# Head-first lanes, T stored by lanes, and weight words moved to ACT's queue in a fused recurrence + two MoE kernel

## The chip, the cores and the metric

One core of a Trainium2 chip runs one program. Times are microseconds (us) on the device. Three runs of the kernel before took 1322.34, 1306.5 and 1322.2 us, median 1322.2. Engines are named as in the profile: PE (TensorE matmul) and PEld (its weight loads), DVE (VectorE), ACT (ScalarE), POOL (GpSimd), and SP, which here only issues DMAs. SP, ACT and POOL each have a queue of their own for the DMAs that they issue.

## The reference, cut to what matters

Three layers run one behind the other on 4 x 768 = 3072 tokens of 320 numbers (8 heads of 40).

```python
for t in range(S):                                   # S = 768, state (B, H, 40, 40) per head
    y[:, :, t] = einsum('bhd,bhde->bhe', rt, state)
    Sa = einsum('bhde,bhe->bhd', state, at)
    state_decay = state * wt[:, :, None, :] - einsum('bhd,bhe->bhde', Sa, bt)
    state = state_decay + einsum('bhd,bhe->bhde', vt, kt)
x = y as tokens (3072, 320)
h = x @ w_in; g = where(h > 0, h, exp(min(h, 0)) - 1); x = g @ w_out      # MoE 1: 320 -> 2048 -> 320
e = argmax(x @ w_gate); p = softmax(x @ w_gate)[e]                        # MoE 2: 8 experts, 320 -> 1024 -> 320
out = p * (relu(x @ w1[e]) @ w2[e])          # up to `capacity` tokens per expert
```

The weights of MoE 1 come as 64-bit numbers. The kernel loads their words and builds a 32-bit number, split in a high part and a low part, on the chip ("conversion").

## The kernel before, in words

**Attention in chunks.** The recurrence is computed in 24 chunks of 32 steps (C), two chunks to a pair p (12 pairs). There are 32 heads over the batch, so a *lane* is one head's 32 steps of one chunk: 128 lanes are the 32 heads of 4 chunks. `lanes(g)` (L126) prepares group g = 0..5, four chunks each: it loads w, a, b and k with 128 lanes on the 128 partitions, multiplies up the decays of w along the 32 steps (L161, L164), the inverse decays (L185, L188), scales a, b and k with them (L169, L191, L196) and stores the results in DRAM (scr_A, scr_W, scr_BK), from where they are read again token by token. Group 0 runs on DVE with room for all four inputs at once, its DMAs on SP's queue; groups 1 to 5 run on POOL with one buffer W and one buffer lx, their DMAs on POOL's queue.

**From lanes to T and U.** `load_tok` (L211) brings tokens of r, a and b/k into two buffers in a fixed order; `pre(p)` (L260) transposes them, multiplies a with b/k into the matrix T of each lane, masks it (L285) and stores it in DRAM (Td, L290). `inverse(p)` (L299) reads T of a pair with 64 lanes on the partitions (TL, L306) and inverts 1 - T in 31 dependent steps of three small DVE operations (L314, L319, L321), stores the inverse in DRAM (Ud, L325) and reads it back as UT (L328). `chain(c, put)` (L363) is the dependent work of a chunk: X from T and the state (copy L390), P from X and UT, the state's update, the output Y (L448), and its transposed tokens.

**MoE 1** (`block`, L567) takes a pair's 256 tokens through w_in and w_out, one pair behind the chain, and `Router.tile` ranks the tokens for MoE 2 and stores them as rows (L699). `Moe1.weights` (L486) makes 40 conversions, 8 times (two w_in tiles, one stacked w_in tile, two w_out tiles). In each, SP loads words into one of three buffers `raw` (L495), ACT takes the absolute value (L499), DVE does four operations (L500 to L503), ACT casts the high part, POOL subtracts it for the low part (L473 by `split`, L510). A w_out conversion is followed by transposes and by a matmul with w_gate on PE (L531, L535). **MoE 2** follows at the end; the change does not touch it.

**What sets the order.** The code is written as generators; `weave` takes steps from several in a given ratio, and a planner then orders the instructions of each engine by priority and by its own picture of time. `ahead(tc, g, n)` gives the steps of g a priority n earlier, `issue_after(i)` keeps a DMA or an instruction behind instruction i in the planner's order. Each engine then runs its list strictly in order, and so does each DMA queue's issuing engine. Before the change, the start (`start`, L1084: lanes 0, pre(0), the loads of chunk 0, lanes 1, the inverse of pair 0, pre(1)) is woven with all 40 conversions 100 to 60 (L1109), behind it comes the loop over pairs.

The dimension order of a lane load, before:

```python
def load(t, x):                                                        # L138
    queue.dma_start(
        flat(t), self.src[x][:, :, 128 * g:128 * g + 128, :].rearrange("b h (c s) d -> c (b h) (s d)", c=4))
```

Of the kernel before, what the change touches and what calls it, by code (L numbers as in the profile page):

```python
# [23 lines left out]
C = 32  # L24
# [14 lines left out]
class Attention:  # L39
# [7 lines left out]
    def __init__(self, ctx, tc, nc, r, k, v, w, a, b):  # L47
# [12 lines left out]
        self.Td = [dr([C, 64, C], f"Td{p}") for p in range(NP)]  # L60
# [65 lines left out]
    def lanes(self, g, eng, eng2=None, room=None):  # L126
# [11 lines left out]
        def load(t, x):  # L138
            queue.dma_start(
                flat(t), self.src[x][:, :, 128 * g:128 * g + 128, :].rearrange("b h (c s) d -> c (b h) (s d)", c=4))  # L140
# [7 lines left out]
        load(w, "w")  # L148
        load(la, "a")
        if room:  # L150
            load(lb, "b")
            load(lk, "k")
# [25 lines left out]
        v = ps[:, 0:128].rearrange("p (c i j) -> p c i j", c=4, j=2)  # L178
# [17 lines left out]
        nc.gpsimd.tensor_tensor(lk, lk, V[:, 1:33, :], ALU.mult)  # L196
# [13 lines left out]

    def load_tok(self):  # L211

        if self.loaded == len(self.order):
            return
        kind, i = self.order[self.loaded]
        t = self.t("tok", self.loaded)
        self.loaded += 1
        for hg in range(2):
            rows = t[64 * hg:64 * hg + 64]
            if kind == "r":  # L220
                self.load_heads(rows, self.src["r"], hg, 64 * i, 64)
            elif kind == "a":
                for cc in range(2):
                    lane = (2 * (i % 2) + cc) * 32 + 16 * hg
                    self.nc.sync.dma_start(
                        rows[32 * cc:32 * cc + 32, :, 0:40],
                        self.scr_A[i // 2][lane:lane + 16].rearrange("l s d -> s l d"))
            else:
                lane = (i % 4) * 32 + 16 * hg
                self.last = self.nc.sync.dma_start(  # L230
                    rows[:, :, 0:40], self.scr_BK[i // 4][lane:lane + 16].rearrange("l x d -> x l d"))
# [28 lines left out]
    def pre(self, p):  # L260
# [13 lines left out]
        for cc in range(2):  # L274
# [24 lines left out]
    def inverse(self, p):  # L299
# [4 lines left out]
        for i in range(2):  # L304
            half = slice(64 * i, 64 * i + 64)
            self.last = self.nc.sync.dma_start(TL[half], self.Td[p].rearrange("s l t -> l s t"))  # L306
            nc.vector.memset(UL[half].rearrange("p a b -> p (a b)")[:, i::34], 1.0)
        yield
        for j in range(31):
# [10 lines left out]
            if m:  # L320
                nc.vector.tensor_tensor(UL[:, 0:n, j + 2:32], UL[:, 0:n, j + 2:32], tv, ALU.add)  # L321
# [15 lines left out]
    def load_bkd(self, c):  # L337
        for hg in range(2):
            lane = (c % 4) * 32 + 16 * hg
            self.nc.sync.dma_start(  # L340
                self.t("BKd", c)[64 * hg:64 * hg + 64], self.scr_BK[c // 4][lane:lane + 16].rearrange("l x d -> x l d"))

    def load_wp(self, c):
        for b in range(4):
            lane = (c % 4) * 32 + 8 * b
            self.nc.sync.dma_start(
                self.t("Wp")[32 * b:32 * b + 32].rearrange("p (h d) -> p h d", h=8),
                self.scr_W[c // 4][lane:lane + 8].rearrange("h s d -> s h d"))
# [127 lines left out]
class Moe1:  # L476
# [9 lines left out]
    def weights(self, pool, route):  # L486
# [5 lines left out]
        def convert(load, m, outs, stacked=False):  # L492
            raw = pool.tile([128, DM, 2], U32, tag="raw", name="raw", bufs=3)
            for q, src in load:
                nc.sync.dma_start(raw.rearrange("p n t -> p (n t)")[:, 0:2 * m].bitcast(U64)[q], src)  # L495
            hi, lo = raw[:, 0:m, 1], raw[:, 0:m, 0]
            xf = route.new_x2()[:, 0:m]
# [6 lines left out]
            if stacked:  # L504
# [10 lines left out]
        every = slice(0, 128)  # L515
        for j in range(FF // n):
            cs = slice(j * n, j * n + n)
            for kt in range(2):
                convert([(every, self.w_in[128 * kt:128 * kt + 128, cs])], n, (self.wiH[:, kt, cs], self.wiL[:, kt, cs]))
                yield  # L520
            convert([(slice(0, 64), self.w_in[256:320, cs]), (slice(64, 128), self.w_in[256:320, cs])], n,
                    (self.wiS[:, cs],), True)
            yield
            for f in (2 * j, 2 * j + 1):
                xf, t = convert([(every, self.w_out[128 * f:128 * f + 128, :])], DM,
                             (self.woH[:, f, 0:DM], self.woL[:, f, 0:DM]))
                with self.tc.high_priority(offset=500):
# [9 lines left out]
                    split(nc, self.woH[:, f, DM:], self.woL[:, f, DM:], ps[:, 384:384 + E])  # L537
                yield
# [78 lines left out]
class Router:  # L617
# [11 lines left out]
    def setup(self):  # L629
        nc, t = self.nc, self.c.tile  # L630
        self.wg = t([128, 3, E], F32, name="wg")
        nc.sync.dma_start(self.wg[:, 0:2, :], self.w_gate[0:256, :].rearrange("(k p) e -> p k e", p=128))
        nc.sync.dma_start(self.wg[0:64, 2, :], self.w_gate[256:320, :])
# [36 lines left out]
    def tile(self, c, o):  # L670
# [28 lines left out]
        nc.sync.dma_start(self.rows.rearrange("(b s) d -> b s d", b=B)[:, C * c:C * c + C, :], x2[:, 0:ROW])  # L699
# [347 lines left out]
def body(ctx, tc, r, k, v, w, a, b, w_in, w_out, w_gate, w1, w2, out, capacity=768):  # L1047
# [35 lines left out]

    def start():  # L1084
# [9 lines left out]
        att.load_pv(0)  # L1094
        att.load_bkd(0)
        att.load_pv(1)
        att.load_wp(0)
        with tc.issue_after(att.last.ins):
            drain(att.lanes(1, nc.gpsimd))
        yield from inverse  # L1100
        yield from att.pre(1)

    def some(g, n):
        for _ in range(n):
            if next(g, 0) == 0:
                return
            yield

    weave((ahead(tc, start(), 1000), 100), (conv, 60))  # L1109
# [90 lines left out]
```

## Time and profile before

| what | us |
|---|---|
| median of three runs | 1322.2 |
| profiled execution | 1325.83 |
| its span | 1324.0 |
| PE busy | 1037.8 |
| DVE busy | 802.2 |
| ACT busy | 598.3 |
| POOL busy | 299.6 |
| first moe1 matmul (L583) begins | 249.7 |
| X copies of the 24 chunks (L390), first and last | 139.7, 954.6 |

Busy time is an average over stages with different limits: it says which engine has the most to do, not what ends the waits in one stage. In a row of the timeline, the number behind the start is the duration, and in brackets stands the idle time of the engine before it with what ended it. In the chain of waits each row is a start, a duration and the work or the wait that held the chain there; "SPq" is SP's queue while it issues. The DMA share is the mean busy share of 16 DMA engines.

### The profile page before, as it was taken

What the parts mean: (1) busy time and instruction counts of PE and PEld (TensorE: products, weight loads), DVE (VectorE), ACT (ScalarE), POOL (GpSimd) and SP (SyncE); (2) the same over time, 40 slices, a digit from 0 to 9 for tenths busy, and PEclk for the clock granted to TensorE, in tenths of its full rate; (3) what the DMA queues carried; (4) which work ended last, traced back from release to release, by engine and by line L of the source; (5) the groups of instructions that cost most, each with busy time, mean ns of one, the idle gap of its engine ahead of it and who ended that gap; (6) DMA issues with size and microseconds to landing.
All of it is one profiled execution on the core that took longest, in us unless ns stands there. A gap on an engine that the chain in (4) does not pass through costs nothing.

```text
span 1324.0 us, 35742 instructions
## 1 busy us (share of the span) xinstructions
PE 1037.8 (78%) x14568; PEld 945.8 (71%) x14568; DVE 802.2 (61%) x2714; ACT 598.3 (45%) x1498; POOL 299.6 (23%) x355
## 2 busy tenths in 40 slices
PE   0144165777769988989899999989989679999994
PEld 0133155666668777878788888889989679889994
DVE  2345675677448864878667686867555425655541
ACT  0233123445425544546455655656656425534430
POOL 4343253454231341021000000000000141232311
PEclk9999996898779988899899999989999879999997
DMA  3767456655563566455452536342130146545210
GB/s 99 167 157 134 114 128 135 139 154 107 134 141 68 112 125 132 68 100 104 68 88 45 90 56 101 53 81 49 28 89 11 35 116 174 138 127 162 76 41 19
DMA packets 325645, 131.27 MB, mean 99 GB/s; under 512 B 292808, under 2 KB 307280, under 8 KB 325472
## 3 DMA queue, kind: packets, MB, share of 16 engines
q1 hardware_dynamic: 304848, 89.24, 34.4%
q0 software_dynamic: 19664, 37.43, 10.1%
q8 instruction: 117, 1.92, 0.7%
q10 hardware_dynamic: 960, 2.23, 0.6%
q14 instruction: 56, 0.46, 0.1%
HBM read 99.13 MB, written 31.00 MB: 98 GB/s over the span
## 4 chain that ended last, share of the span: by engine, by line
DMA 27%; PE 24%; DVE 23%; issue 11%; ACT 3%; POOL 3%; SPq 2%; another core or an unknown queue 0%; ACTq 0%; POOLq 0%; DVEq 0%
DMA W<-in_w_dram 5%; PE ps_h L583 4%; DMA out_dram<-ys,ids 4%; DVE ut L314 3%; DVE inv L319 3%; DMA inv<-Td 3%; DVE inv L321 3%; PE ps_c L375 3%; DMA lx<-in_k_dram 2%; DMA raw<-in_moe_w_in_dram 2%; DMA Ud<-inv 2%; DVE ST L421 2%; PE ps_c L903 2%; PE ps_h L903 2%; DVE e L589 2%
## 5 line engine op out<-in xcount | busy, mean ns | idle before, releaser
L472 ACT CAST gH<-e 128x256 fp32r<-128x256 f32 x192 | 77.0, 405 | 136.0 <-DVE e L589 128.4
L597 PE MATMUL ps_o<-woH,gH 128*128 128x328 f32 x384 | 130.2, 341 | 9.6 <-ACT gH L472 9.6
L599 PE MATMUL ps_o<-woH,gL 128*128 128x328 f32 x384 | 120.7, 336 | 8.3 <-DVE gL L473 8.2
L598 PE MATMUL ps_o<-woL,gH 128*128 128x328 f32 x384 | 126.0, 330 | 0.0
L583 PE MATMUL ps_h<-xH,wiH 128*128 128x256 f32 x368 | 112.5, 307 | 13.4 <-DVE e L589 12.6
L700 POOL DMA_INDIRECT list<-ids,idx x24 | 24.6, 1026 | 429.9 <-DVE idx L698 322.0
L589 DVE SCALAR_TENSOR_TENSOR e<-e,ps_h 128x256 f32<-128x256 f32 x184 | 76.5, 417 | 60.5 <-ACT e L588 58.2
L314 DVE TENSOR_TENSOR ut<-inv 128x30 f32<-128x30 f32 (+4 forms) x360 | 95.1, 264 | 26.9 <-DMA inv<-Td 26.5
L583 PE MATMUL ps_h<-xL,wiH 128*128 128x256 f32 x368 | 109.7, 298 | 0.0
L583 PE MATMUL ps_h<-xH,wiL 128*128 128x256 f32 x368 | 109.0, 296 | 0.0
L473 DVE TENSOR_TENSOR gL<-e,gH 128x256 fp32r<-128x256 f32 x192 | 81.5, 429 | 30.2 <-ACT gH L472 26.8
L319 DVE SCALAR_TENSOR_TENSOR inv<-inv 128x1 f32<-128x1 f32 (+15 forms) x372 | 98.1, 264 | 0.5
L321 DVE TENSOR_TENSOR inv<-inv,ut 128x30 f32<-128x30 f32 (+4 forms) x360 | 96.0, 267 | 0.3
L587 ACT ACTIVATE e<-ps_h 128x256 f32<-128x256 f32 x184 | 70.7, 384 | 54.4 <-PE ps_h L583 35.2
L244 PE MATMUL ps_p<-ident,tok 128*104 128x128 f32 x288 | 55.5, 321 | 41.0 <-DMA tok<-scr_A 15.4
L583 PEld LDWEIGHTS ps_h<-xH,wiH 128*128 128x128 f32 x368 | 73.7, 201 | 18.7 <-DVE e L589 17.6
L597 PEld LDWEIGHTS ps_o<-woH,gH 128*128 128x128 f32 x384 | 77.6, 202 | 12.0 <-ACT gH L472 10.7
L599 PEld LDWEIGHTS ps_o<-woH,gL 128*128 128x128 f32 x384 | 73.8, 200 | 10.7 <-DVE gL L473 9.7
L588 ACT ACTIVATE e<-e 128x256 f32<-128x256 f32 x192 | 79.1, 416 | 4.1
L598 PEld LDWEIGHTS ps_o<-woL,gH 128*128 128x128 f32 x384 | 77.8, 203 | 0.2
L583 PEld LDWEIGHTS ps_h<-xL,wiH 128*128 128x128 f32 x368 | 74.6, 203 | 0.1
L583 PEld LDWEIGHTS ps_h<-xH,wiL 128*128 128x128 f32 x368 | 74.2, 202 | 0.0
(308 smaller groups left out, 2882.4 us busy)
## 6 DMA issues: line engine op xcount, KB each, us to landing
r<-in_moe_w_dram SPq DMA_DIRECT2D x15, 640.0 KB
tok<-scr_BK SPq DMA_DIRECT2D x48, 160.0 KB
BKd<-scr_BK SPq DMA_DIRECT2D x48, 160.0 KB
r<-in_moe_w_dram SPq DMA_DIRECT2D x7, 1024.0 KB
W<-in_w_dram POOLq DMA_DIRECT2D x10, 640.0 KB
scr_BK<-lx POOLq DMA_DIRECT2D x10, 640.0 KB
inv<-Td SPq DMA_DIRECT2D x24, 256.0 KB
raw<-in_moe_w_out_dram SPq DMA_DIRECT2D x16, 320.0 KB
```

What stands on the lines that cost most here:

```text
L314: nc.vector.tensor_tensor(tv, TL[:, j:j + 1, j + 2:32].to_broadcast([128, n, m]), UL[:, 0:n, j:j + 1].to_broadcast([128, n, m]), ALU.mult,)
L319: nc.vector.scalar_tensor_tensor(col, UL[:, 0:n, j], TL[:, j, j + 1:j + 2], col, ALU.mult, ALU.add)
L321: nc.vector.tensor_tensor(UL[:, 0:n, j + 2:32], UL[:, 0:n, j + 2:32], tv, ALU.add)
L472: split.last = nc.scalar.copy(H, x)
L473: return (low or nc.vector).tensor_tensor(L, x, H.bitcast(F32), ALU.subtract)
L583: nc.tensor.matmul(h, l, r, start=i == 0, stop=i == len(seq) - 1)
L587: nc.scalar.activation(e, h, AF.Relu, scale=-1.0)
L588: nc.scalar.activation(e, e, AF.Exp, scale=-1.0)
L589: nc.vector.scalar_tensor_tensor(e, e, -1.0, h, ALU.add, ALU.max)
L597: nc.tensor.matmul(o, gH[:, ts], self.woH[:, f], start=f == 0, stop=False)
L598: nc.tensor.matmul(o, gH[:, ts], self.woL[:, f], start=False, stop=False)
L599: nc.tensor.matmul(o, gL[:, ts], self.woH[:, f], start=False, stop=f == NF - 1)
```

## The change

The change does four things.

- A lane group puts the four chunks of one head on neighbouring partitions (lane = 4 * head + chunk instead of 32 * chunk + head). The loads of w, a, b and k then have (b h) as their slowest dimension; all later reads of scr_A, scr_W and scr_BK take every fourth lane (`of`). In group 0, w and b go on SP's queue, k and a on ACT's. Its scaling of k runs on DVE (`eng2`), not on POOL.
- T is kept in DRAM lane by lane (Td is 64 lanes, s, t), so that the scatter is in the store and not in the load. UT comes back in four loads for each chunk instead of one, and the rows of a routed tile go out in four stores instead of one.
- The words of the weights (and w_gate) are loaded on ACT's queue, three buffers ahead. The low part is subtracted on DVE, and every third conversion has a buffer of its own.
- The first three word loads are set behind ACT's copy that reads k; nine conversions stand behind the scaling of k, ahead of the first inverse, and 31 behind the end of the first inverse. pre(1) is woven with those 31.

```diff
-        self.Td = [dr([C, 64, C], f"Td{p}") for p in range(NP)]
+        self.Td = [dr([64, C, C], f"Td{p}") for p in range(NP)]
@@ lanes
-                flat(t), self.src[x][...].rearrange("b h (c s) d -> c (b h) (s d)", c=4))
+                flat(t), self.src[x][...].rearrange("b h (c s) d -> (b h) c (s d)", c=4))
...
-        load(w, "w")
-        load(la, "a")
         if room:
-            load(lb, "b")
-            load(lk, "k")
+            for q, t, x in ((nc.sync, w, "w"), (nc.sync, lb, "b"), (nc.scalar, lk, "k"), (nc.scalar, la, "a")):
+                q.dma_start(
+                    flat(t), self.src[x][...].rearrange("b h (c s) d -> (b h) c (s d)", c=4))
+            self.landed = nc.scalar.copy(self.t("WCd")[:, 40:41], lk[:, 0, 0:1])
+        else:
+            load(w, "w")
+            load(la, "a")
...
-        nc.gpsimd.tensor_tensor(lk, lk, V[:, 1:33, :], ALU.mult)
+        self.scaled = eng2.tensor_tensor(lk, lk, V[:, 1:33, :], ALU.mult)
...
+    def of(self, t, c, first, n):
+        return t.rearrange("(l c) s d -> c l s d", c=4)[c, first:first + n]
@@ load_tok
+                with self.tc.issue_after(self.returned.ins) if i == 4 else ExitStack():
+                    self.last = self.nc.sync.dma_start(
+                        rows[:, :, 0:40], self.of(self.scr_BK[i // 4], i % 4, 16 * hg, 16).rearrange("l x d -> x l d"))
@@ pre
-                    self.Td[p][:, 32 * cc + 16 * hg:32 * cc + 16 * hg + 16, :].rearrange("s l t -> s (l t)"),
-                    TM[64 * hg:64 * hg + 32, :])
+                    self.Td[p][32 * cc + 16 * hg:32 * cc + 16 * hg + 16].rearrange("l s t -> s l t"),
+                    TM[64 * hg:64 * hg + 32, :].rearrange("s (l t) -> s l t", t=C))
@@ inverse
-            self.last = self.nc.sync.dma_start(TL[half], self.Td[p].rearrange("s l t -> l s t"))
+            self.last = self.nc.sync.dma_start(TL[half], self.Td[p])
...
-            self.nc.sync.dma_start(
-                self.t("UT", 2 * p + cc).rearrange("p h t -> p (h t)"),
-                self.Ud[p][:, 32 * cc:32 * cc + 32, :].rearrange("s (b h) t -> b s (h t)", b=4))
+            for b in range(4):
+                h = 32 * cc + 8 * b
+                self.returned = self.nc.sync.dma_start(
+                    self.t("UT", 2 * p + cc)[32 * b:32 * b + 32], self.Ud[p][:, h:h + 8, :])
@@ Moe1.weights
-                nc.sync.dma_start(raw.rearrange("p n t -> p (n t)")[:, 0:2 * m].bitcast(U64)[q], src)
+                    nc.scalar.dma_start(raw.rearrange("p n t -> p (n t)")[:, 0:2 * m].bitcast(U64)[q], src)
...
-                nc.gpsimd.tensor_tensor(H[r], xf[r], Hs[r].bitcast(F32), ALU.subtract)
+                nc.vector.tensor_tensor(H[r], xf[r], Hs[r].bitcast(F32), ALU.subtract)
             else:
-                split(nc, *outs, xf, nc.gpsimd)
+                split(nc, *outs, xf)
@@ Router.tile
-        nc.sync.dma_start(self.rows.rearrange("(b s) d -> b s d", b=B)[:, C * c:C * c + C, :], x2[:, 0:ROW])
+        for b in range(B):
+            at = S * b + C * c
+            nc.sync.dma_start(self.rows[at:at + C, :], x2[C * b:C * b + C, 0:ROW])
@@ body
-    weave((ahead(tc, start(), 1000), 100), (conv, 60))
+    first = ahead(tc, start(), 1000)
+    for _ in range(26):
+        next(first)
+    with tc.issue_after(att.landed.ins):
+        next(conv)
+    weave((first, 20), (behind(att.scaled.ins, some(conv, 9)), 20))
+    weave((ahead(tc, att.pre(1), 1000), 10), (behind(att.inverted.ins, conv), 40))
```

The planner decides where the pieces land, so the order of three places is shown. SP's queue at the very start, before (names: inv, lx and keep hold w, a, then b and k; raw holds words):

```order
L139 DMA inv<-in_w_dram 128x1x1280
L139 DMA lx_144<-in_a_dram 128x1x1280
L139 DMA keep<-in_b_dram 128x1x1280
L139 DMA keep<-in_k_dram 128x1x1280
L632 DMA wg<-in_moe_w_gate_dram 128x2x8
L633 DMA wg<-in_moe_w_gate_dram 64x8
L495 DMA raw<-in_moe_w_in_dram 128x256 x2
L208 DMA pv_151<-in_v_dram 32x16x40 x2
L208 DMA pv_152<-in_v_dram 32x16x40 x2
L495 DMA raw<-in_moe_w_in_dram 64x256 x2
L145 DMA scr_A_89<-lx_144 64x1280 x2
```

and SP's queue now:

```order
L151 DMA inv<-in_w_dram 128x1x1280
L151 DMA keep<-in_b_dram 128x1x1280
L145 DMA scr_A_89<-lx_144 64x1280 x2
L145 DMA scr_BK_101<-keep 64x1280 x4
L233 DMA tok_149<-scr_A_89 32x16x40 x4
L681 DMA list<-BKd_175 128x200
L239 DMA tok_150<-scr_BK_101 64x16x40 x2
L145 DMA scr_W_95<-W_143 64x1280 x2
```

Two of the lane loads, w_gate, the words and the loads of v have left the head of SP's queue: the stores of lanes 0 and the first token loads follow directly. DVE at the end of lanes 0, before (x_240 and x_253 are conversions, L191 scales b):

```order
L188 TENSOR_TENSOR inv<-inv 128x320
L500 SCALAR_TENSOR_TENSOR x_240<-x_240,raw 128x256
L188 TENSOR_TENSOR inv<-inv 128x320
L500 SCALAR_TENSOR_TENSOR x_253<-x_253,raw 128x256
L501 TENSOR_SCALAR raw<-x_240 128x256
L188 TENSOR_TENSOR inv<-inv 128x320
L501 TENSOR_SCALAR raw<-x_253 128x256
L502 SCALAR_TENSOR_TENSOR x_240<-x_240,raw 128x256
L188 TENSOR_TENSOR inv<-inv 128x320
L502 SCALAR_TENSOR_TENSOR x_253<-x_253,raw 128x256
L503 SCALAR_TENSOR_TENSOR x_240<-raw,x_240 128x256
L191 TENSOR_TENSOR keep<-keep,inv 128x1280
```

and now (L201 scales k, x_324 is the first conversion):

```order
L190 TENSOR_TENSOR inv<-inv 128x4x40
L193 TENSOR_TENSOR inv<-inv 128x320 x4
L196 TENSOR_TENSOR keep<-keep,inv 128x1280
L201 TENSOR_TENSOR keep<-keep,inv 128x1280
L516 SCALAR_TENSOR_TENSOR x_324<-x_324,raw 128x256
```

The lane work of group 0 is now in one piece, and the first conversion begins behind it. DVE at the beginning of the first inverse, before:

```order
L314 TENSOR_TENSOR ut_179<-inv 128x30
L319 SCALAR_TENSOR_TENSOR inv<-inv 128x1
L502 SCALAR_TENSOR_TENSOR x_415<-x_415,raw 128x256
L321 TENSOR_TENSOR inv<-inv,ut_179 128x30
L314 TENSOR_TENSOR ut_180<-inv 128x29
L503 SCALAR_TENSOR_TENSOR x_415<-raw,x_415 128x256
L319 SCALAR_TENSOR_TENSOR inv<-inv 128x1
L473 TENSOR_TENSOR woL<-ps_r,woH 128x8
L321 TENSOR_TENSOR inv<-inv,ut_180 128x29
```

and now:

```order
L481 TENSOR_TENSOR woL<-ps_r,woH 128x8
L323 TENSOR_TENSOR ut_179<-inv 128x30
L328 SCALAR_TENSOR_TENSOR inv<-inv 128x1
L330 TENSOR_TENSOR inv<-inv,ut_179 128x30
L323 TENSOR_TENSOR ut_180<-inv 128x29
L328 SCALAR_TENSOR_TENSOR inv<-inv 128x1
L330 TENSOR_TENSOR inv<-inv,ut_180 128x29
```

The steps of the first inverse follow each other with no conversion among them. The first X copy of a chunk, which had 16 conversions begun ahead of it on DVE, now has 12, and stands behind the whole inverse, not in its last third. On POOL the subtractions are gone, and the loads and products of lanes 1 stand right behind the setup.

## Rows read from the trace of the kernel before

**Rows 1.** Windows: busy us (count) of PE, PEld, DVE, ACT, POOL; clock; DMA share; GB/s.
```profile
0.00:165.00 165.00, 42.05 (x331) 33.22 (x331) 78.88 (x253) 37.98 (x90) 61.19 (x101) 1.00 0.59 135
165.00:410.00 245.00, 173.33 (x2788) 156.69 (x2789) 158.33 (x498) 99.22 (x271) 99.53 (x116) 0.83 0.60 129
...
570.00:970.00 400.00, 371.90 (x7019) 339.27 (x7023) 287.73 (x1132) 231.12 (x614) 23.65 (x21) 0.97 0.41 70
```

**Rows 2.** The chain of waits, longest pieces in order of time: start, us, what.
```profile
51.15 2.91 SPq L230
54.11 5.21 SPq L230
...
60.80 4.80 DMA scr_W<-W
66.17 13.09 DMA W<-in_w_dram
...
88.72 2.92 DVE raw L501
...
108.95 17.89 DMA raw<-in_moe_w_out_dram
...
142.87 3.78 DMA raw<-in_moe_w_in_dram
...
169.95 17.32 DMA W<-in_w_dram
...
208.19 17.05 DMA raw<-in_moe_w_in_dram
...
302.63 16.42 DMA W<-in_w_dram
...
562.93 3.65 DMA Ud<-inv
```

**Rows 3.** Windows, two stretches of the start: the last two columns are DMA share and GB/s.
```profile
4.00:12.00 8.00, 0.00 (x0) 0.00 (x0) 0.00 (x0) 0.00 (x0) 7.74 (x18) 1.00 0.25 77
46.00:48.00 2.00, 0.47 (x2) 0.45 (x3) 1.44 (x4) 1.27 (x3) 0.88 (x1) 1.00 0.91 201
```

**Rows 4.** Timeline from 12 to 44 us, lanes 0: start, us, instruction, idle before.
```profile
12.48 0.24 DVE L159 COPY W<-inv 128x160 f32<-128x160 f32 x1 [11.49 <-DMA inv<-in_w_dram]
...
18.88 2.88 POOL L169 TENSOR_TENSOR lx<-lx,W 128x1280 f32<-128x1280 f32 x1 [6.77 <-DMA lx<-in_a_dram]
19.04 3.07 DVE L188 TENSOR_TENSOR inv<-inv 128x320 f32<-128x320 f32 x1
...
37.91 5.06 POOL L196 TENSOR_TENSOR keep<-keep,inv 128x1280 f32<-128x1280 f32 x1 [14.67 <-DVE inv L188]
...
38.41 1.49 DVE L191 TENSOR_TENSOR keep<-keep,inv 128x1280 f32<-128x1280 f32 x1
```

**Rows 5.** Timeline of DVE in the first inverse: its start, one step, its end.
```profile
103.81 0.19 DVE L314 TENSOR_TENSOR ut<-inv 128x30 f32<-128x30 f32 x1 [4.70 <-DMA inv<-Td]
...
110.69 0.26 DVE L314 TENSOR_TENSOR ut<-inv 128x110 f32<-128x110 f32 x1
...
111.19 0.26 DVE L314 TENSOR_TENSOR ut<-inv 128x105 f32<-128x105 f32 x1
...
144.69 0.25 DVE L319 SCALAR_TENSOR_TENSOR inv<-inv 128x16 f32<-128x16 f32 x1
```

**Rows 6.** Timeline of PE at 165 us; the UT loads' issues by line (ns min/median/max).
```profile
165.37 0.89 PE L375 MATMUL ps_c<-X,UT 32*32 32x40 f32 x40 [6.89 <-DMA UT<-Ud]
...
L328 SPq DMA_DIRECT2D UT<-Ud x24: 530/554/695, 152.7 to 919.3; - x24
```

**Rows 7.** To 410 us: conversions' tile (DVE third), low-part subtraction by line, SP's waits.
```profile
0.00:410.00 410.00, 19.48 (x96) 18.85 (x96) 79.58 (x160) 29.89 (x80) 6.64 (x8) 0.90 0.59 131
...
L473 DVE TENSOR_TENSOR gL<-e,gH 128x256 fp32r<-128x256 f32 x28 | 12.3, 446 | 0.4 <-PE ps_o L599 0.4
...
SPq L495 <- PE ps_r L535: 22.9, 3, 10.7
```

More of the change, by code (lines that the diff above doesn't have):

```diff
@@ L490, in weights, with fetch, convert @@
         least = float(np.uint32(0x38100000).view(np.float32))
-        def convert(load, m, outs, stacked=False):
-            raw = pool.tile([128, DM, 2], U32, tag="raw", name="raw", bufs=3)
-            for q, src in load:
-                nc.sync.dma_start(raw.rearrange("p n t -> p (n t)")[:, 0:2 * m].bitcast(U64)[q], src)
+        def fetch():
+            if todo:
+                loads, m = todo.pop(0)
+                raw = pool.tile([128, DM, 2], U32, tag="raw", name="raw", bufs=3)
+                for q, src in loads:
+                    nc.scalar.dma_start(raw.rearrange("p n t -> p (n t)")[:, 0:2 * m].bitcast(U64)[q], src)
+                here.append(raw)
+        def convert(m, outs, stacked=False):
+            raw = here.pop(0)
             hi, lo = raw[:, 0:m, 1], raw[:, 0:m, 0]
-            xf = route.new_x2()[:, 0:m]
+            third = len(todo) % 3 == 0
+            xf = (pool.tile([128, DM], F32, tag="xf", name="xf", bufs=1) if third else route.new_x2())[:, 0:m]
             xi = xf.bitcast(U32)
@@ L509, in convert @@
                 r = slice(64, 128)
-                nc.gpsimd.tensor_tensor(H[r], xf[r], Hs[r].bitcast(F32), ALU.subtract)
+                nc.vector.tensor_tensor(H[r], xf[r], Hs[r].bitcast(F32), ALU.subtract)
             else:
-                split(nc, *outs, xf, nc.gpsimd)
+                split(nc, *outs, xf)
             return xf, raw.rearrange("p n t -> p (n t)").bitcast(F32)
         every = slice(0, 128)
+        todo, here = [], []
+        for j in range(FF // n):
+            cs = slice(j * n, j * n + n)
+            todo += [([(every, self.w_in[128 * kt:128 * kt + 128, cs])], n) for kt in range(2)]
+            todo.append(([(slice(0, 64), self.w_in[256:320, cs]), (slice(64, 128), self.w_in[256:320, cs])], n))
+            todo += [([(every, self.w_out[128 * f:128 * f + 128, :])], DM) for f in (2 * j, 2 * j + 1)]
+        for _ in range(3):
+            fetch()
+        yield
         for j in range(FF // n):
@@ L537, in weights @@
                     split(nc, self.woH[:, f, DM:], self.woL[:, f, DM:], ps[:, 384:384 + E])
+                fetch()
                 yield
@@ L631, in setup @@
         self.wg = t([128, 3, E], F32, name="wg")
[L632 to L633 removed]
+        nc.scalar.dma_start(self.wg[:, 0:2, :], self.w_gate[0:256, :].rearrange("(k p) e -> p k e", p=128))
+        nc.scalar.dma_start(self.wg[0:64, 2, :], self.w_gate[256:320, :])
         self.down = t([128, E], F32, name="down")
@@ L1082, in body, with some @@
     route.empty_list(att.t("BKd").rearrange("p a b -> p (a b)").bitcast(I32))
+    def some(g, n):
+        for _ in range(n):
+            if next(g, 0) == 0:
+                return
+            yield
     def start():
@@ L1093, in start, with behind @@
         next(inverse)
[L1094 to L1097, printed above, removed]
         with tc.issue_after(att.last.ins):
-            drain(att.lanes(1, nc.gpsimd))
-        yield from inverse
[L1101 to L1106, printed above, removed]
-            yield
-    weave((ahead(tc, start(), 1000), 100), (conv, 60))
+            att.load_pv(0)
+            att.load_bkd(0)
+            att.load_wp(0)
+            att.load_pv(1)
+        yield
+        drain(att.lanes(1, nc.gpsimd))
+        yield from inverse
+    def behind(ins, g):
+        while True:
+            with tc.issue_after(ins):
+                if next(g, 0) == 0:
+                    return
+            yield
+    first = ahead(tc, start(), 1000)
[5 more added lines that the diff above has]
+    weave((ahead(tc, att.pre(1), 1000), 10), (behind(att.inverted.ins, conv), 40))
     lanes = None
```

29 lines of the change are left out of this document (12 added, 17 removed).

## The prediction, made before the changed kernel was run

> **What bounds the kernel now.** I read the busy time by stretches first, then the chain of waits, then the timeline of the start. The stretches [rows 1] show three kernels in one. From 570 to 970 us TensorE is busy 372 of 400 us: nothing but TensorE work can be saved there. Before 165 us it works 42 us, and from 165 to 410 us 173 of 245 us at a granted clock of 0.83. So the time to be had lies ahead of about 410 us, and what ends the waits there is in the chain of waits [rows 2]: loads of the lanes stage (W from w, 13.09, 17.32, 16.42 us), words of the weights (17.89 and 17.05 us), and SP's own issuing (2.91 and 5.21 us for two loads). The same view prices an unhindered DMA: 4.80 us for the store of W, 640 KB in two halves, and 3.78 us for a load of words.
>
> Why the lane loads take so long is in the share of the DMA engines [rows 3]: from 4 to 12 us only lane loads are under way and the 16 engines are busy 0.25, that is four of them; between 46 and 48 us, with stores and token loads under way, 0.91. In the code the lane loads have c=4 as the slowest dimension in DRAM, the stores 64 rows. The Trainium skill, "DMA: Bandwidth & Descriptors", section "Why a DMA increments its semaphore by 16 and not by 1", says that a copy runs on the largest number of engines up to 16 that divides the slowest dimension of both sides; by that rule 4 becomes 16 in the change, and the UT loads (b=4 slowest) and the stores of routed rows gain likewise. The trace agrees on the 0.25; nothing in it shows these loads on 16.
>
> **The change part by part.** *First loads.* w lands at 12.48, a at 18.88 us [rows 4]: 6.40 us for 640 KB on four engines, so packets begin near 6.1 us. On all engines it is 1.6 us each; w on SP's queue shares them with k on ACT's, so w lands near 9.3.
>
> *Lanes of stage 0 on DVE.* From w to the last inverse decays DVE needs 6.6 us to 19.04, then 3.07 for an operation that runs beside POOL's 2.88 us, three more like it (a quarter of the elements of the 1.49 us product, about 0.4 each), and the two products of b and k at 1.49 each, the second of which moves from POOL [rows 4]. That is 23.2 us. Before it was POOL's end, 37.91 + 5.06 = 43.0, because the order put conversions between these operations, and they waited for words queued behind the lane loads. Gain 19.8.
>
> *To the first inverse.* It begins at 103.81 [rows 5], 60.8 us after that end. Of this I take away three things in [rows 2]: SP's blocked issue of the two token loads (8.1), the excess of the W load of lanes 1 over the unhindered store (13.09 - 4.80 = 8.3; the second pair of token loads waits beside it on the same engines), and the conversion step of 2.92 us on DVE in front of the mask of T. 23.2 + 60.8 - 19.3 = 64.7. Bounds: nothing goes (84.0), or the conversions' other waits go as well (about 55, with 10 us more of the 60.8). I take the named pieces alone.
>
> *The first inverse.* It runs 103.81 to 144.94, 41.1 us, with conversions among its 31 steps that wait for words (17.89 us in the chain). A step that nothing disturbs takes 0.50 us [rows 5], so 15.5 us in all. POOL's inverse decays of lanes 1 fall in it now, seven products of 160 columns, four of 320 and one of 1280: by elements 2.9 times its 2.88 us product [rows 4], 8.3 us. The row at 19.04 shows a DVE product of a quarter of that size drawn out to POOL's own length; but POOL's 5.06 us for a product that took 2.88 shows that it yields too. I take 6: 21.5 us, end at 86.2. The Trainium skill, "SBUF — State Buffer", section "SBUF: two separate sides", says that DVE and GpSimd share a pair of ports as a lock, and whoever comes second is blocked for the whole instruction. By it all 8.3 count, and the sum below is 2.3 us worse.
>
> *Back from DRAM.* From its end to the matmul with UT at 165.37 [rows 6] pass 20.4 us. The store of U unhindered takes 3.65 [rows 2], and I take as much for the UT load; issuing takes 0.55 us each [rows 6], two for U and eight instead of two for UT, and 0.7 for the first gap: 13.5. With token loads ahead in SP's queue I take 15 (bounds 13.5 and 20.4 + 3.3). First use at 101.2 instead of 165.4: **-64**, between -40 and -76.
>
> *T by lanes* trades a scattered read for a scattered store. The store is now of the kind of U's store (128 bytes each, 3.65 us), half the bytes; the read has whole 4 KB rows. I cost it at nothing: in the front it lies in the stretch from the mask to the inverse, which I left as it was, and after 570 us TensorE's 372 of 400 hides it. Without that cover, 2 us either way for each of 12 pairs.
>
> *Word loads on ACT's queue.* 48 issues move; at 0.55 us they are 27 us of ACT, which is idle 146 of the 245 us to 410 [rows 1]. Nothing, if they don't wait. ACT's first copy waits for k, with nothing but the words behind it. SP loses these 48 and gains 72 for UT and 72 for rows; only the six on the first UT path count, above. The token load of chunk 4 is set behind the UT loads; behind it on SP stand the stores and the load of pair 1's T, which no term above waits for. The layout of lanes moves no compute.
>
> *After the first use.* Four lane loads stand in the chain from 169.95 to 302.63 us, the first 17.32, the last 16.42 [rows 2]; at 16 each against 4.8 that is 45, and the words' 17.05 against 3.78 another 13. Chains shift when a wait goes, so I take half of 58: **-29** (0 to -58). Against it, DVE's own work. A conversion costs 79.6 / 40 = 2.0 us there and its low part, moved from POOL, 0.446 for 256 columns [rows 7]: 40 of these are some 18 us, 31 of them behind the inverse 14. The order puts 12 conversions ahead of the first X copy instead of 16: four more, 8 us. So 22 us more for a DVE that is busy 158 of 245 [rows 1]; idle time covers part, I take half: **+10** (0 to 22).
>
> Sum: -64 - 29 + 10 = -83. The profiled execution took 1325.8 (span 1324.0); the median shown, 1322.2, is 3.6 below. 1325.8 - 83 - 3.6 = **1239 us**.
>
> **The rivals.**
> - *More is freed than I count.* All 58 of the lane waits go, and TensorE, less interrupted, holds its level of 2.4 GHz rather than 1.2 for more of the stretch (0.83 now, 0.97 later [rows 1]: its 173 us would be 148, -25). -64 - 58 + 10 - 25 = -137: 1185. For it: the lane loads slow every other queue too. Against: the conversions must still be paid before block 0 ends.
> - *Given back.* The front gains 64, but DVE becomes the bound of the next stretch, with 31 conversions: no lane wait shows, and all 22 count: -42, 1280. For it: DVE is the engine with most to do per step there. It decides when DVE is busy above 85% from the first UT use to the fifth pair.
> - *The loads don't spread.* They stay on four engines whatever comes first; then only the conversions' removal from the inverse remains, 41.1 - 21.5 = 19.6 us, and the words' 13: -33, 1289. Against it: the 64-row stores at 0.91 [rows 3].
> - *Slower: ACT is held.* A fetch of words waits until its buffer is free, and this wait, SP's until now, stands in front of everything on ACT. Three such waits for the matmul of a w_out conversion took 22.9 us [rows 7], 7.6 each. One for each of the 16 w_out conversions is 122 us; if all reach the path, -83 + 122 = +39: 1361. It decides once ACT's waits at these fetches, on the path, exceed 83 us. Against: ACT has 146 us idle, and the order issues a fetch behind the conversion that frees the buffer.
>
> **How the numbers follow.** Chances: the forecast 0.55 (its own range 1210 to 1265, from the bounds of its three terms taken mostly together), more freed 0.15 (1170 to 1210), given back 0.17 (1265 to 1300), not spread 0.05, ACT held 0.05, something else 0.03. The range 1186 to 1290 leaves out the rival on ACT, the ends of three others and the rest, some 0.18. Measured runs of this kernel lie 1.2% apart, so 2% is about what can be told: faster means under 1296. From the cases: 0.55 + 0.15 + 0.15 + 0.03 = 0.88 faster, 0.08 within (the tops of given back and not spread, part of the rest), 0.04 slower.
>
> **What would show it.** Right: the share of the DMA engines near 0.9 in the first loads; the first inverse begins near 65 and lasts under 25 us without a conversion in it; the first UT matmul near 101; lane loads in the chain at 5 us or gone. Wrong: an inverse that begins after 85 (tokens, not loads, held the front); lane loads still at 13 us; ACT waiting at fetches for tens of us; or a stretch to the tenth chunk that grows by what the front gained.

## The result, and the profile after

Four runs of the changed kernel took 1217.03, 1217.92, 1224.1 and 1223.77 us, median 1220.85, beside 1322.27 for the kernel before: ratio 0.9254, interval 0.9172 to 0.9335. A second series gave 1217.6 and 0.9277 (0.9219 to 0.9336). All ratios compare fast runs alone: in the series that has the run with the lanes chunk-first, two of the seven runs of the kernel before (1323.17 and 1326.94 us) count as slow and are left out. The profiled execution took 1217.03 us (span 1215.3), 108.8 less than the one of before. I had said 1239, in a range of 1186 to 1290, faster: the time lies 18 us below the forecast, inside the forecast's own range of 1210 to 1265.

The busy times by stretches of the kernel after answer to [rows 1, 3]; the columns are the same (PE, PEld, DVE, ACT, POOL; clock; DMA share; GB/s):

```profile
4.00:12.00 8.00, 0.00 (x0) 0.00 (x0) 4.38 (x14) 1.89 (x3) 7.74 (x14) 1.00 1.00 375
...
0.00:165.00 165.00, 72.39 (x894) 59.05 (x894) 114.90 (x334) 48.23 (x118) 84.69 (x132) 0.68 0.74 197
...
165.00:410.00 245.00, 216.51 (x3583) 192.69 (x3583) 206.37 (x680) 134.85 (x366) 65.83 (x79) 0.90 0.59 135
570.00:970.00 400.00, 369.69 (x6086) 342.16 (x6086) 265.16 (x1034) 233.36 (x623) 24.04 (x25) 0.97 0.34 61
```

Three things are to be seen. The first loads run at a DMA share of 1.00 and 375 GB/s, where it was 0.25 and 77. To 410 us TensorE is busy 72 + 217 us, where it was 42 + 173. From 570 to 970 us TensorE is as full as before, 370 of 400 us.

The granted clock is not among them. From 165 to 410 us it is 0.90, not 0.83, but to 165 us it is 0.68, not 1.00, and it differs between two executions of the changed kernel. These are the first 410 us of the kernel before, of the changed kernel, and of the changed kernel in its second series, then 60 to 140 us of the last two:

```profile
0.00:410.00 410.00, 215.38 (x3119) 189.91 (x3120) 237.21 (x751) 137.21 (x361) 160.72 (x216) 0.90 0.59 131
0.00:410.00 410.00, 288.90 (x4476) 251.74 (x4477) 321.27 (x1013) 183.07 (x483) 150.51 (x210) 0.81 0.65 160
0.00:410.00 410.00, 289.97 (x4481) 252.12 (x4481) 323.17 (x1014) 183.29 (x484) 149.41 (x210) 0.92 0.66 160
...
60.00:140.00 80.00, 41.36 (x470) 33.78 (x473) 55.17 (x193) 21.15 (x50) 41.65 (x49) 0.50 0.77 197
60.00:140.00 80.00, 40.56 (x451) 33.24 (x453) 56.58 (x191) 21.13 (x50) 40.91 (x49) 1.00 0.79 193
```

From 60 to 140 us the clock was at the lower of its two levels (1.2 GHz) in the one execution and at the upper (2.4 GHz) in the other; TensorE had been busy 14 and 16 of the 60 us before. Its busy time there, 41.36 and 40.56 us, and the X copy of chunk 1, at 153.1 and 152.85 us, are nearly the same. So a lower clock in this stretch cost nothing that can be seen.

The chain of waits to 420 us (start, us, what) answers to [rows 2]:

```profile
0.81 6.54 DMA inv<-in_w_dram
...
28.15 6.33 DMA tok<-scr_A
...
42.28 4.31 DMA raw<-in_moe_w_in_dram
...
61.49 3.79 DMA Td<-keep
...
65.86 4.66 DMA inv<-Td
...
93.78 7.49 DMA Ud<-inv
101.78 2.38 DMA UT<-Ud
...
106.94 8.99 DMA Td<-keep
116.50 8.85 DMA inv<-Td
...
146.43 5.45 DMA raw<-in_moe_w_in_dram
...
213.86 7.85 DMA raw<-in_moe_w_in_dram
```

After the first load no load of lanes is left in it, and the longest load of words is 7.85 us, not 17.89. What stands there now is T and U on their way through DRAM. The timeline of DVE shows the first inverse, as [rows 5] did before, and the one of TensorE the first matmul with UT, as [rows 6]:

```profile
70.55 0.19 DVE L323 TENSOR_TENSOR ut<-inv 128x30 f32<-128x30 f32 x1 [5.38 <-DMA inv<-Td]
...
72.74 2.85 DVE L328 SCALAR_TENSOR_TENSOR inv<-inv 128x2 f32<-128x2 f32 x1
...
92.86 0.24 DVE L328 SCALAR_TENSOR_TENSOR inv<-inv 128x16 f32<-128x16 f32 x1
...
104.30 0.31 PE L383 MATMUL ps_c<-X,UT 32*32 32x40 f32 x2 [6.87 <-DMA UT<-Ud]
```

The inverse runs from 70.55 to 93.10 (before 103.81 to 144.94), and the first UT use comes at 104.30, 61.1 us earlier.

### The profile page after: what moved, and what is told of

Same layout as the page of the kernel before. It is cut to its first block, busy times and chain, and to the rows that moved or that the text cites. A ratio compares the mean times of both kernels' runs of the same rounds, so it can differ in the third digit from the quotient of the medians.

```text
span 1215.3 us, 35896 instructions
## 1 busy us (share of the span) xinstructions
PE 1027.2 (85%) x14568; PEld 933.5 (77%) x14568; DVE 822.6 (68%) x2755; ACT 599.1 (49%) x1499; POOL 256.1 (21%) x314
## 4 chain that ended last, share of the span: by engine, by line
PE 41%; DVE 27%; DMA 19%; ACT 5%; issue 5%; SPq 2%; POOL 1%; ACTq 0%; POOLq 0%; DVEq 0%
PE ps_h L609 8%; PE ps_c L383 4%; DVE inv L328 4%; DVE inv L330 4%; DVE ut L323 3%; DMA out_dram<-ys,ids 3%; DMA inv<-Td 3%; PE ps_o L623 3%; PE ps_o L625 3%; PE ps_o L624 3%; PE ps_c L931 2%; DMA Td<-keep 2%; PE ps_h L931 2%; DMA r<-in_moe_w_dram 2%; DMA Ud<-inv 2%
## 5 line engine op out<-in xcount | busy, mean ns | idle before, releaser
L328 DVE SCALAR_TENSOR_TENSOR inv<-inv 128x1 f32<-128x1 f32 (+15 forms) x372 | 101.5, 273 | 0.6
L330 DVE TENSOR_TENSOR inv<-inv,ut 128x30 f32<-128x30 f32 (+4 forms) x360 | 99.7, 277 | 0.2
L253 PEld LDWEIGHTS ps_p<-ident,tok 128*104 128x104 f32 x288 | 35.9, 148 | 56.4 <-issue 25.5
```

The lines of the kernel that those rows point to most:

```text
L253: self.nc.tensor.transpose(ps[0:104, 128 * j:128 * j + 128], t[:, 2 * q:2 * q + 2, :].rearrange("p a e -> p (a e)")[:, 0:104], self.ident,)
L328: nc.vector.scalar_tensor_tensor(col, UL[:, 0:n, j], TL[:, j, j + 1:j + 2], col, ALU.mult, ALU.add)
L330: self.inverted = nc.vector.tensor_tensor(UL[:, 0:n, j + 2:32], UL[:, 0:n, j + 2:32], tv, ALU.add)
```

## The experiments

"After" is the changed kernel, and its row is its second series. Ratios are to the kernel before, run beside each on the same chip; X(0) and X(7) are the starts of the X copies of chunks 0 and 7 in the profiled execution, and the last column is TensorE's busy time in its first 410 us.

| kernel | median us | ratio, interval | X(0), X(7) | PE to 410 |
|---|---|---|---|---|
| before, five series | 1309.2 to 1322.3 | 1 | 140, 463 | 215.4 |
| after | 1217.6 | 0.9277, 0.9219 to 0.9336 | 94, 378 | 290.0 |
| after, lanes chunk-first | 1335.3 | 1.0178, 1.0086 to 1.0269 | 133, 474 | 217.2 |
| before, lanes head-first | 1235.75 | 0.9397, 0.9281 to 0.9512 | 100, 403 | 273.8 |
| before, group 0 head-first | 1318.31 | 1.0052, 1.0017 to 1.0088 | 121, 468 | 230.4 |
| before, groups 1 to 5 head-first | 1247.79 | 0.9507, 0.9446 to 0.9568 | 122, 410 | 261.3 |
| after, chunk-first in four DMAs | 1246.77 | 0.9517, 0.9456 to 0.9579 | 101, 391 | 279.4 |
| after, order of conversions as before | 1222.71 | 0.9324, 0.9241 to 0.9407 | 103, 391 | 275.7 |
| after, words on SP's queue | 1228.0 | 0.9357, 0.9262 to 0.9453 | 97, 378 | 282.8 |
| the same, 19 copies on 4 engines | 1279.58 | 0.974, 0.9682 to 0.9798 | 120, 438 | 242.7 |
| the same, 19 copies on 16 engines | 1244.22 | 0.9468, 0.942 to 0.9516 | 99, 396 | 273.8 |
| after, T, UT and rows as before | 1209.27 | 0.9232, 0.917 to 0.9294 | 94, 373 | 284.9 |
| after, low parts on POOL | 1219.47 | 0.93, 0.9227 to 0.9374 | 96, 378 | 290.3 |

**The yardstick.** The changed kernel as it is, in the second series (the row "after").

> The changed kernel once more, to stand beside the other runs on one chip: 1217 to 1225 by every theory.

**Lanes chunk-first in the changed kernel.** In all lane loads, in the transposed last decays and in `of`:

```diff
-... .rearrange("b h (c s) d -> (b h) c (s d)", c=4))
+... .rearrange("b h (c s) d -> c (b h) (s d)", c=4))
-        return t.rearrange("(l c) s d -> c l s d", c=4)[c, first:first + n]
+        return t.rearrange("(c l) s d -> c l s d", c=4)[c, first:first + n]
```

> The changed kernel with one part undone: lanes are chunk-first again (lane = 32 * chunk + head, the chunk slowest in DRAM), everything else as changed. Theory (the loads spread because of their slowest dimension): the DMA share in the first loads falls from about 0.9 to 0.25; w lands near 12 to 19 us instead of 7.4, each later lane load takes 13 to 17 us again instead of about 4.5, the first inverse begins 10 to 25 us later and lane loads stand in the chain of waits again: 30 to 55 us lost, 1250 to 1275. Rival (the gain is the place of the conversions, the loads are hidden): under 12 us lost, 1233 or less. Second rival (loads spread whatever comes first): the share stays at 0.9 and nothing is lost.

It lost 115 to 118 us, twice what I expected at most, and is 1.8% slower than the kernel before. Windows of its first loads, and its chain of waits:

```profile
6.00:10.00 4.00, 0.00 (x0) 0.00 (x0) 0.00 (x0) 0.00 (x0) 4.00 (x5) 1.00 0.26 103
```

```profile
16.14 17.59 DMA raw<-in_moe_w_in_dram
...
61.89 14.23 DMA W<-in_w_dram
...
90.19 21.00 DMA W<-in_w_dram
...
176.26 15.07 DMA raw<-in_moe_w_in_dram
```

The share is 0.26 again, and the words wait as long as the lanes, although on ACT's queue only two lane loads now stand ahead of them. Its last conversion begins at 366.6 us (before 311.1). So without the new loads the rest of the change gains nothing. That it is slower than before because 31 conversions, with their slow words, stand behind the first inverse is likely but not shown: the queues, the form of T and the low parts differ from the kernel before too.

**Head-first lanes alone, in the kernel before.** The same lines the other way, with `of` added; queues and order stay.

> The kernel before with one part alone: head-first lanes (loads, reads of scr_A, scr_W, scr_BK and the view of the last decays), all queues, the words and the order of the conversions as before. Theory: w lands near 8.5 us instead of 12.5, W of lanes 1 takes about 5 us instead of 13, the four later lane loads about 5 instead of 16: 35 to 60 us gained, 1262 to 1287. Rival (place of the conversions): 10 us or less gained, 1312 to 1322.

79 us gained of about 95, above the 35 to 60 that I had expected. The place of the conversions is not what carries the change.

**Which loads.** The same edit with a condition on the group:

```diff
-... .rearrange("b h (c s) d -> c (b h) (s d)", c=4))
+... .rearrange("b h (c s) d -> (b h) c (s d)" if g == 0 else "b h (c s) d -> c (b h) (s d)", c=4))
```

> The kernel before with head-first lanes in group 0 alone (the loads of the start); groups 1 to 5, on POOL, stay chunk-first. Theory (the lead at the first X copy is mostly lost again, since the run with the old order of the conversions lost 28 us of lead by chunk 1 and had it back by chunk 7; what counts is how fast lanes 1 and 2 and the conversions get done): 0 to 20 us gained, 1295 to 1315. Rival (my sum: the front is on the path): first X copy 25 us or more earlier and 25 to 40 us gained, 1275 to 1290.

> The kernel before with head-first lanes in groups 1 to 5 alone; group 0 stays chunk-first. Theory (the loads on POOL's queue carry it): 50 to 75 us of the 79 that head-first gained in all, 1240 to 1265. Rival (my sum, which gave the later lane loads half of 45 and the W load of lanes 1 8.3): 25 to 40 gained, 1275 to 1290.

Group 0 alone gains nothing, not even the little that I had expected (5 us lost), though the first X copy comes 19 us earlier. Groups 1 to 5 alone gain 65, as the theory said. In these two runs the first X copy comes at the same time, at 121 and 122 us, and they end 70 us apart. The chain of waits of the run with group 0 alone shows where its lead went:

```profile
86.90 23.92 DMA raw<-in_moe_w_out_dram x2
...
131.54 12.50 DMA lx<-in_k_dram
...
149.39 16.68 DMA W<-in_w_dram
...
188.90 17.55 DMA Ud<-inv
...
230.23 12.50 DMA Td<-keep
...
246.78 14.96 DMA raw<-in_moe_w_in_dram
```

The reader is to see not the two lane loads but their neighbours. U's store, T's store and the words go through SP's queue, and the lane loads through POOL's. Yet U takes 17.55 us, where it took 3.65 late in the kernel before [rows 2] and 7.49 in the changed kernel.

**Is it the number of engines?** The changed kernel with chunk-first lanes and each load in four DMAs, each with 32 heads slowest:

```diff
-            queue.dma_start(
-                flat(t), self.src[x][:, :, 128 * g:128 * g + 128, :].rearrange("b h (c s) d -> (b h) c (s d)", c=4))
+            for c in range(4):
+                queue.dma_start(
+                    flat(t[32 * c:32 * c + 32]),
+                    self.src[x][:, :, 128 * g + 32 * c:128 * g + 32 * c + 32, :].rearrange("b h s d -> (b h) (s d)"))
...
```

> The changed kernel with chunk-first lanes as in the run that lost 115 us, but each lane load cut into four DMAs, one for each chunk, so that 32 heads are the slowest dimension of each; layout in DRAM and all reads of the lanes stay chunk-first. Theory (the slowest dimension sets the number of DMA engines, and that is all that head-first does): DMA share in the first loads back near 0.9, W of lanes 1 in 4 to 6 us, 1217 to 1240 (18 more issues a group on POOL's or SP's and ACT's queue). Rival (head-first gains by how the stored lanes are read back, or by the order the planner then chooses): little comes back, 1300 or more.

Of the 118 us, 89 came back without a change to the layout in DRAM; the time is 7 us above my range. Windows of the first loads of this kernel, and of the changed kernel in the same series:

```profile
6.00:10.00 4.00, 0.00 (x0) 0.00 (x0) 0.63 (x1) 0.05 (x1) 4.00 (x5) 1.00 1.04 213
```

```profile
6.00:10.00 4.00, 0.00 (x0) 0.00 (x0) 2.57 (x7) 0.76 (x2) 4.00 (x5) 1.00 1.02 390
```

Both keep all engines busy, but the four DMAs move 213 GB/s and the one 390. Each of the four goes to 32 partitions only. The Trainium skill, "SBUF — State Buffer", section "Door 1: The DMA port swizzle", says that 32 partitions reach half of the 16 ports on the memory's side, and that a transfer to them gets about half the rate; the ratio here, 0.55, agrees. That the remaining 29 us come from this alone was not tried.

**Does a load on four engines harm the others?** The changed kernel with the words on SP's queue, with copies that nobody waits for on ACT's queue (by its condition the edit makes 19 of them, not the 20 of the expectations):

```diff
+            if len(todo) % 2:
+                with self.tc.issue_after(first.ins):
+                    nc.scalar.dma_start(
+                        self.att.spare.pop().rearrange("(c l) x -> c l x", c=4),
+                        self.att.src["w"][:, :, 0:128, :].rearrange("b h (c s) d -> c (b h) (s d)", c=4))
```

> The changed kernel with the words on SP's queue (1228 us as measured), plus 20 copies of 640 KB from w in DRAM to spare DRAM, one behind every second conversion on ACT's queue, where nothing else stands between the start and chunk 8. Nobody reads or waits for them. They have the four chunks slowest, as the lane loads had before. Theory A (a load on four engines harms every other DMA, because each of those also needs these four): loads of words, T and U stand in the chain at 12 to 18 us, first in the stretch to 275 us, and the time is 35 to 90 us above the twin with 16 engines. Theory B (a slow lane load harms by its own landing only, for which POOL waits): within 12 us of the twin.

The twin has `"(l c) x -> l c x"` and `"b h (c s) d -> (b h) c (s d)"`.

> The twin of the run with spare copies: the same 20 copies of the same bytes at the same places, with the 32 heads slowest. By both theories it prices the bytes and the issues alone (20 issues of 0.55 us, and 1.6 us of all engines for each copy by the first loads): 0 to 25 us above the 1228 without copies, 1228 to 1253.

The copies cost 16 us on 16 engines and 52 on four: 35 us for the same bytes, at the lower end of what theory A said, and for copies on which nothing depends. The chain of waits of the run on four engines, and of its twin:

```profile
60.88 21.04 DMA raw<-in_moe_w_out_dram
...
125.94 14.14 DMA raw<-in_moe_w_out_dram
...
179.54 11.70 DMA raw<-in_moe_w_in_dram
...
203.12 10.87 DMA Td<-keep
```

```profile
43.61 6.13 DMA raw<-in_moe_w_in_dram
...
58.16 4.84 DMA Td<-keep
...
63.57 10.32 DMA inv<-Td
...
174.99 8.83 DMA Ud<-inv
```

Waits for words of 12 to 21 us stand in the first, although the copies are in another queue. Inside the wait of 21.04 us, from 60.88 to 81.92, lies this stretch of the run on four engines:

```profile
75.50:78.50 3.00, 0.00 (x0) 0.00 (x0) 0.00 (x0) 0.00 (x0) 2.61 (x6) 1.00 0.26 104
```

A share of 0.26 is about four engines' worth, and the rest of the 16 engines' time is unused while the words wait. Of it the copies in ACT's queue take 13.5%, the DMAs in POOL's queue 11.1%, and those in SP's, the words among them, 1.0%. SP's issuing is held as well: one load of words, at 70.96 us, took it 7.03 us to issue. Theory B is out. The Trainium skill, "DMA: Bandwidth & Descriptors", section "Why a DMA increments its semaphore by 16 and not by 1", says that a DMA is complete only when each engine that it runs on has finished its part; the waits of words beside copies on four engines agree with that.

**Order of the conversions.** Start and first inverse woven with all conversions 100 to 60 again:

```diff
-    weave((first, 20), (behind(att.scaled.ins, some(conv, 9)), 20))
-    weave((ahead(tc, att.pre(1), 1000), 10), (behind(att.inverted.ins, conv), 40))
+    def then():
+        yield from first
+        yield from ahead(tc, att.pre(1), 1000)
+    weave((then(), 100), (conv, 60))
```

> The changed kernel with the order of the conversions undone: start and the first inverse are woven with all 40 conversions 100 to 60 as before, no conversion is set behind the scaling of k or behind the end of the inverse; layout, queues and low parts as changed. Theory: lanes 0 are still done near 23 us, but conversions stand inside the first inverse, which lasts 30 to 40 us instead of 22, and the first X copy comes 10 to 25 us later; part of it comes back since those conversions are then done: 8 to 20 us lost, 1229 to 1241. Rival (the spread of the loads is all): under 5 us either way.

The first inverse ended at 120 instead of 93 us and X(1) came 28 us later; by chunk 7 it was 12, and the ratio differs by 0.5% inside both intervals. The conversions were done at 225 instead of 275 us: what the first chunks lose, the next ones get back. The 2 to 6 us of the measurement lie near the rival's number (under 5) and below the theory's (8 to 20), though the first X copies moved as the theory said.

**Words on SP's queue**, with `nc.sync` for `nc.scalar` at the fetch and w_gate:

> The changed kernel with the words of the weights and w_gate back on SP's queue, fetched three buffers ahead at the same places of the program. Theory (the words waited for the lane loads on four engines, not for SP): with loads spread, a load of words lands within 4 to 8 us on either queue, and the time stays within 10 us, 1211 to 1231. Rival (SP is the queue that is full: 48 more issues of 0.55 us, some of them ahead of the loads of UT and of tokens): waits for words of 15 us or more stand in the chain again, and 12 to 30 us are lost, 1233 to 1251.

0.8% slower, as the theory allowed; the intervals overlap. No wait for words over 7.53 us stands in its chain to 420 us.

**T, UT and rows as before** (the three hunks on them taken back):

> The changed kernel with its three smaller changes of DMAs undone together: T in DRAM step by step (scattered in the load again), UT in one load for each chunk, routed rows in one store for each chunk; head-first lanes, queues and the order of the conversions as changed. Theory (these loads are on the path only in the first 100 us, where a lead is not kept, and TensorE's work hides them after chunk 8): within 8 us of the changed kernel, 1210 to 1226. Rival (four engines instead of 16 cost the UT loads and the stores of rows 5 us or more each, and the chain of a chunk waits for UT): 12 us or more lost, above 1230, and DMA of UT in the chain at 8 us or more.

A shade faster than the changed kernel; the intervals overlap, so it isn't told apart. The rival is out.

**Low parts on POOL** (`split(nc, *outs, xf, nc.gpsimd)` and the stacked one likewise):

> The changed kernel with the low parts of the conversions subtracted on POOL again, as before. Theory (up to chunk 6 DVE is the engine with the most to do, 83% busy from 101 to 410 us; my sum gave the move of the low parts a cost of up to 18 us of DVE's time): 5 to 15 us gained, 1203 to 1213. Rival (POOL's operation is longer than the 0.45 us it takes on DVE, draws out the DVE operation beside it, and holds the lanes): nothing gained or up to 12 lost, 1218 to 1230.

Nothing gained: the rival.

## Why the prediction came out right, and which of its steps did not

**First loads, lanes 0, first inverse, way back: right in size.** w landed at 7.35 us (I said 9.3), lanes 0 were done at 22.4 (23.2), the inverse began at 70.55 (64.7) and lasted 22.5 us (21.5), and the first UT use came at 104.3 (101.2). The share of the first loads is 1.00, which agrees with the rule on the slowest dimension in the Trainium skill, "DMA: Bandwidth & Descriptors", section "Why a DMA increments its semaphore by 16 and not by 1". On the way back two errors met: the store of U took 7.49 us for the 3.65 I gave it, and the eight UT loads 2.38 for 3.65 and more.

The inverse took 7 us more than 31 undisturbed steps at 0.50 us, where I had added 6, but the pieces are others than those I had priced. POOL's timeline, with two of the DVE operations beside it:

```profile
64.69 4.11 POOL L190 TENSOR_TENSOR W<-W 128x160 f32<-128x160 f32 x7 [1.87 <-DMA W<-in_w_dram]
69.82 2.73 POOL L193 TENSOR_TENSOR W<-W 128x320 f32<-128x320 f32 x3
70.79 0.88 DVE L330 TENSOR_TENSOR inv<-inv,ut 128x30 f32<-128x30 f32 x1
72.63 2.94 POOL L196 TENSOR_TENSOR lx<-lx,W 128x1280 f32<-128x1280 f32 x1
...
85.94 2.93 POOL L201 TENSOR_TENSOR lx<-lx,W 128x1280 f32<-128x1280 f32 x1 [4.36 <-DMA lx<-in_k_dram]
86.04 2.96 DVE L330 TENSOR_TENSOR inv<-inv,ut 128x96 f32<-128x96 f32 x1
```

The seven products of 160 columns, a part of my 8.3 us, were over before the inverse began. Four products fell in it, 7.7 us in all: the last two of 320 columns, the scaling of b, and that of k, which I had not counted. Each held one small DVE operation for about its own length (0.88, 0.87, 2.85 and 2.96 us, where such an operation takes about 0.2 beside no product), and that cost 6.7 us. Three operations of conversions ahead of the last step, from 91.79 us on, cost 1 more, the mask of the next T (76.73 us) 0.6, and the steps without these took 14.2 us, not 15.5. By the Trainium skill, "SBUF — State Buffer", section "SBUF: two separate sides", whoever comes second is blocked for the whole instruction; the trace agrees, and that my 6 came near the 7 is luck.

**The step that the runs bear out only in part: -64 as a part of the sum.** I took the lead at the first UT use for time at the end. In the changed kernel the lead does last: its X copies come 46 us earlier at chunk 0, 84 at chunk 7 and 89 at the last. But a lead at the start does not last by itself. With group 0 alone a lead of 19 us at chunk 0 was 3 at chunk 5, and with the old order of the conversions 9 to 28 us that were lost on the first chunks left no measurable loss. Where the later loads are fast too, group 0's lead is kept: with all groups head-first the X copies come 22 us ahead of those with groups 1 to 5 alone at chunk 0, 7 at chunk 7 and 21 at the last, and the times differ by 14 (79 less 65), though the two intervals do not tell that from nothing. So the front's worth depends on the stage to chunk 7, which must also make 40 conversions and read lanes 1, and each of these went through DMAs that stood beside lane loads. My sum added the two stages as if they were independent.

**The step that was mis-sized: -29 after the first use.** "Chains shift when a wait goes, so I take half of 58." The lane loads of groups 1 to 5, with the W load of lanes 1 (8.3 us of my -64), are worth 65 us alone. More than the waits that I summed went. The runs with spare copies give a reason: a load on four engines makes the DMAs of other queues late, and I had priced only its own landing and the words behind it. Nineteen such copies cost 35 us by that alone, and groups 1 to 5 have 20 lane loads of the same size, though at other times and into on-chip memory, so about half of the 65 is a rough estimate for it; how the 65 divide was not measured. I had this as a word in favour of the rival in which more is freed.

That the sum of -83 came near the measured -101 is in part luck: the front counts for less by itself and the later loads for more, DVE's +10 was not there, and 19 us that the kernel gained behind the last X copy stand in no term.

**DVE's extra, +10: not seen.** From the first UT use to the first X copy of the fifth pair, 104.3 to 414 us, DVE is busy 254.14 of 309.7 us, 82%, just under the 85% at which I let the rival "given back" decide; with the low parts on POOL again nothing changed. **T by lanes and the words' queue, nothing: held** within what can be told. **ACT held: out.** None of the 48 issues at the fetch shows idle time of ACT ahead of it.

**The lead in numbers that last.** TensorE works through much the same work in every run, and from chunk 8 on it is nearly always busy (146 of 160 us from 410 to 570 us), so what counts is how much it had done by then. The table's last column orders the runs roughly as their times do: 215 to 243 us in the four kernels above 1275 us, 261 to 290 in those below 1250. The clocks of these profiles differ (0.72 to 0.92 over these 410 us), so the number of matmuls is the safer count; it orders them alike: 2950 to 3662 in the four, 4071 to 4638 in the others, most in the fastest. The first X copy does not: it comes 7 us earlier than before with the lanes chunk-first, the slowest kernel, and at the same time in the two runs of one part of the groups each. The last X copy orders them well, from 837 us in the fastest to 970 in the slowest, but not us for us: with T, UT and rows as before it comes 30 us earlier than in the second profile of the changed kernel (867), and the spans, 1209.9 and 1220.5, differ by 11. The rival in which more is freed came true in part: the profiles stand 109 us apart where it said 137. That the clock gave a part of this is not shown, since two executions of the changed kernel, with clocks of 0.81 and 0.92 to 410 us, took 1217.03 and 1222.27 us.

**Open.** The 16 us between head-first lanes alone and the whole change are split between order, queue and the rest in parts too small to be told apart; the order (6), the queue (10), the forms (-6) and the low parts (3) are each inside their intervals. From the last X copy to the end the kernel before took 369 us and the one after 350; about 12 of these us lie in the last blocks of MoE 1 and 8 in MoE 2, and no run was made for that.

## What to carry to other kernels

Look at the DMA share while one load is alone. A share that is a simple fraction of all engines (0.25 here) is a sign that the load's shape, not its size, sets its time: 32 in the slowest place instead of 4 brought it to 1.00, and was worth 79 of the 95 us, more than any change of order or queue in this kernel. Such a load can also delay the DMAs of other queues, so count the neighbours' late landings, not its own wait alone. And before a lead at the start goes into a sum, ask what the work behind it must still pay before the next engine is full.

## What the runs showed of the hardware that I had not expected

- Nineteen copies of 640 KB that nobody waits for cost 35 us more on four engines than on sixteen, and loads of words in another queue then took up to 21.04 us.
- Four loads of 32 partitions each kept the DMA share at 1.04 and moved 213 GB/s, where one load of 128 partitions moved 390 at 1.02: a full share is not a full rate.
- A DVE operation of two columns took 2.85 us beside a POOL product of 2.94 us that began 0.11 us ahead of it; the four POOL products in the first inverse held one DVE operation each, and the rest ran at their usual 0.2 us.
- With TensorE's clock at 1.2 GHz in one execution and 2.4 GHz in another from 60 to 140 us, its busy time there was 41.36 and 40.56 us.
